# A pool of its own for the first attention, with eleven more buffers for coded weights and a deeper decode lead

## The chip, the cores and the metric

The kernel runs on one core of one Trainium2 chip. The metric is the device time of one execution in microseconds (us). Times are given as the median of several executions; the trace comes from one profiled execution of its own.

## What is computed

Attention with a decaying bias over 2 batches, 8 heads and 576 positions; then a feed-forward layer with an ELU-like activation (2048 hidden); then a mixture of four experts (1024 hidden each) weighted by normalised probabilities.

```python
cum = np.cumsum(np.maximum(s, 0.0), axis=-1)
bias = -(cum[:, :, :, None] - cum[:, :, None, :])
scores = np.where(causal, -1e9, q @ k.T / 8 + np.minimum(bias, 0.0))
x = softmax(scores) @ v                      # 1152 tokens x 512
h = x @ w_in                                 # w_in 512 x 2048
x = np.where(h > 0, h, np.exp(np.minimum(h, 0)) - 1) @ w_out
p = probs / (probs.sum(-1, keepdims=True) + 1e-9)
out = sum(p[:, e:e+1] * (np.maximum(x @ w1[e], 0) @ w2[e]) for e in range(4))
```

## The kernel before

The 1152 tokens are worked in three groups of 256, 448 and 448 (`GROUPS`). The weights come in **units** of 128 hidden columns: a unit is a tile of 128 x 1024, its first 512 columns the block of the up matrix and its last 512 the block of the down matrix. The feed-forward layer has 16 units (`NAB`), the four experts 8 each (`NCD`), 32 in all.

The 16 units of the feed-forward layer arrive as 64-bit integers (`w64`), that is as 32 **coded halves** of 512 KB, each half a unit. `fetch_halves` (L118) issues their loads on the queue of the SP engine (SyncE), in the order of `order` (L103), into buffers borrowed from tags whose real use comes later. `turn` (L106) lists these: one `wu` tile with two halves, three `gt` tiles, and then rounds of `small` with eleven halves (`yh`, `yl`, three `raw`, three in `xa`, three in `ox`). The first sixteen halves so find a free buffer at once; a half of a later round waits until the half before it in the same buffer is decoded. `decode_halves` (L131) turns a half into 32-bit weights with two ScalarE operations (L146, L148) and two VectorE operations (L149, L151), and sends each finished unit to a DRAM tile (`w_dec`, L154, on the GpSimd queue) for the later groups. `DEC` (L46) gives how many halves are decoded at four points within the first attention; afterwards `advance(n)` (L592) decodes up to half 2n + `AHEAD` in slot n.

The first group's attention (`attention_first`, L234) takes only its first 256 positions and stands ahead of everything. It begins with 12 unread products of the identity with itself (`keep_warm`, L330); an fp32 product is two instructions on TensorE. `scores`, `probabilities`, `normalise`, `transposes` and `values` follow for four pairs of heads. `transposes` and `keep_warm` take turns in two PSUM buffers (`ps_att`).

Then `layer1(0, ...)` (L667) runs the feed-forward layer on group 0 in plain fp32, one slot for each unit: `up1`, exponential (L699), `Relu` (L702) and VectorE step (L703) into `gt`, `advance`, and two slots later `down1`. Its PSUM buffers for `up1` are two, so `up1` of slot k waits for L703 of slot k - 2. After slot 3 `sums_hook` calls `cum_parts` (L191), which writes the running sums and their parts to DRAM on ScalarE's DMA queue; its tile `rows` has one buffer and is filled and written twice.

From slot 14 on a `Background` interleaves the attention of group 1 (`attention_parts`, L365): `load_small` and `load` (under `late`, which puts their DMAs behind the last load of a coded half) and `split` (L431), whose loads from `rows_d` (L443, L444) are not under `late`. Then the 32 expert units follow for group 0 (`up2`, `down2`), with `fetch` (L91) four units ahead on the SP queue into `raw`, and `prepare` (L95). Groups 1 and 2 come after that. Each engine and each DMA queue works its instructions in order; the framework's scheduler sets that order, starting from the order of the program but moving instructions forward where it takes an engine to be free.

Of the kernel before, what the change touches and what calls it, by code (L numbers as in the profile page):

```python
# [9 lines left out]
F32R = mybir.dt.float32r  # L10
# [6 lines left out]
B, H, S, D = 2, 8, 576, 64  # L17
# [25 lines left out]
BG_FROM = [14, 0, 0]  # L43
BG_TO = [1, 1, 0]

DEC = [1, 2, 3, 4]  # L46
AHEAD = 6

N_WU, N_GT = 1, 3

@with_exitstack
def tile_kernel(ctx, tc, qT, kT, v, s, w64, w, probs, out):
    nc = tc.nc


    base = ctx.enter_context(tc.tile_pool(name="base", bufs=1, reuse_waits="tile"))

    edge = ctx.enter_context(tc.tile_pool(name="edge", bufs=1, side="right"))
    att_stack, l1_stack = ExitStack(), ExitStack()
    att_pool = att_stack.enter_context(tc.tile_pool(name="att", bufs=1, reuse_waits="tile"))  # L60
    l1_pool = l1_stack.enter_context(
        tc.tile_pool(name="l1", bufs=1, side="right", reuse_waits="tile"))
    psum = ctx.enter_context(tc.tile_pool(name="ps", bufs=1, space=bass.MemoryType.PSUM))
    PE, DVE, ACT, POOL, SP = nc.tensor, nc.vector, nc.scalar, nc.gpsimd, nc.sync
# [5 lines left out]

    def sb(shape, tag, bufs, dtype=F32):
        p = (base if tag in BASE else edge if tag in EDGE else l1_pool if tag in L1
             else att_pool)
        return p.tile(shape, dtype, tag=tag, name=tag, bufs=bufs)

    def ps(tag, bufs):
# [26 lines left out]
    order = [(0, 0)] + [h for n in range(NAB - 1) for h in ((n + 1, 0), (n, 1))] + [(NAB - 1, 1)]  # L103

    small = [("yh", 1, 1), ("yl", 1, 1)] + [("raw", 3, 1)] * 3 + [("xa", 1, 3), ("ox", 1, 3)]
    turn = [("wu", 5, 2)] * N_WU + [("gt", 3, 1)] * N_GT + small * 4  # L106
    places = [(tag, bufs, n, i) for tag, bufs, n in turn for i in range(n)]
    coded, freed_by, last_in = {}, [], {}
    for i, (tag, bufs, many, k) in enumerate(places):
# [81 lines left out]
    def cum_parts():  # L191

        ACT.dma_start(out=cum_d, in_=cum)
        one = sb([B * H, S], "bias", 2)
        POOL.memset(one, 1.0)
        for i in (2, 3):
            ACT.dma_start(out=rows_d[:, i], in_=one)
        for i, sign in ((0, 1.0), (4, -1.0)):
            t = sb([B * H, 2, S], "rows", 1, F32R)
            ACT.activation(t[:, 0], cum, AF.Copy, scale=sign)  # L200
            DVE.scalar_tensor_tensor(out=t[:, 1], in0=cum, scalar=sign, in1=t[:, 0].bitcast(F32),
                                     op0=ALU.mult, op1=ALU.subtract)
            ACT.dma_start(out=rows_d[:, i:i + 2], in_=t.bitcast(F32))
# [30 lines left out]
    def attention_first(x):  # L234


        n = 256
        qkv = sb([128, 3, 4, n], "pt", 2)
        SP.dma_start(out=s_sb, in_=s)
        for c in (0, 2):  # L240
            for i, t in enumerate((qT, kT)):
                SP.dma_start(out=qkv[:, i, c:c + 2], in_=t[0, 128 * c:128 * c + 256, 0:n]
                             .rearrange("(c p) n -> p c n", p=128))
        fetch_halves(1)
        vv = qkv[:, 2].rearrange("p c n -> p (c n)").rearrange("p (c d) -> p c d", c=2)
        SP.dma_start(out=vv, in_=v[0, 0:n].rearrange("(c p) d -> p c d", p=128))
        fetch_halves()
        cum_sums()
        pp = []
        for tag, heads in (("k2", 3), ("k2", 3), ("q2", 1), ("q2", 1)):  # L250
            t = sb([128, heads, 3 * 128], tag, 2)
            pp += [t[:, h] for h in range(heads)]
        ptt = sb([128, H, 3 * 128], "pt", 2)
        sm = sb([128, 2, H], "sm8", 1)


        parts, less = (sb([80, n], t, 1, F32R) for t in ("cump", "cumm"))
        ones = sb([80, B * H], "ones", 1, F32R)
        POOL.tensor_copy(ones[:64], ident[:64, :B * H])
        POOL.tensor_copy(ones[64:], ident[64:80, 64:64 + B * H])  # L260
        for t, sign in ((parts, 1.0), (less, -1.0)):
            POOL.tensor_copy(t[:64], zero)
            ACT.activation(t[:B * H], cum[:, 0:n], AF.Copy, scale=sign)
            DVE.scalar_tensor_tensor(out=t[64:], in0=cum[:, 0:n], scalar=sign,
                                     in1=t[:B * H].bitcast(F32), op0=ALU.mult, op1=ALU.subtract)

        chunks = [(0, 128), (128, 256)]  # L270
        banks = {}

        def scores(hp):
            for j in range(2):
                h = 2 * hp + j
                banks[h] = ps(f"acc{h % 4}", 1) if h < 4 or h > 5 else ps("up", 2)
            for d0, d1 in chunks:
                for j in range(2):
                    r = slice(64 * j, 64 * j + 64)
                    PE.matmul(banks[2 * hp + j][:, d0:d0 + d1], qkv[r, 0, hp, d0:d1],  # L280
                              qkv[r, 1, hp, 0:d1], start=d0 == 0, stop=False,
                              skip_group_check=True)
            for j in range(2):
                h = 2 * hp + j
                one = ones[:, h:h + 1]
                for d0, d1 in chunks:
                    o = banks[h][:, d0:d0 + d1]
                    PE.matmul(o, one.to_broadcast([80, 128]), parts[:, 0:d1],
                              start=False, stop=False, skip_group_check=True)
                    PE.matmul(o, less[:, d0:d1], one.to_broadcast([80, d1]),  # L290
                              start=False, stop=d0 > 0, skip_group_check=True)

        def probabilities(hp):
            for j in range(2):
                h = 2 * hp + j
                for i, (d0, d1) in enumerate(chunks):
                    p = pp[h][:, d0:d0 + d1]
                    nm = sb([128, 1], "nm", 8)
                    DVE.tensor_tensor_reduce(p, banks[h][:, d0:d0 + d1], mask[:, S - d1:],
                                             -1.0 / SC, 3.0e38, ALU.add, ALU.min, nm)  # L300
                    ACT.activation(p, p, AF.Exp, bias=nm, scale=-1.0, accum_out=sm[:, i, h:h + 1])

        def normalise(hp):
            r = sm[:, :, 2 * hp:2 * hp + 2]
            DVE.tensor_scalar(r, r, 1e-9, None, op0=ALU.add)
            DVE.reciprocal(r, r)
            for h in (2 * hp, 2 * hp + 1):
                for i, (d0, d1) in enumerate(chunks):
                    p = pp[h][:, d0:d0 + d1]
                    scaled = DVE.tensor_scalar(p, p, sm[:, i, h:h + 1], None, op0=ALU.mult)  # L310
            return scaled

        def transposes(hp):
            for h in (2 * hp, 2 * hp + 1):
                pt = ps_att()
                for m in range(3):
                    ms = slice(128 * m, 128 * m + 128)
                    PE.transpose(pt[:, ms], pp[h][:, ms], ident)
                ACT.activation(ptt[:, h], pt[:, :384], AF.Copy)

        def values(hp):
            o = ps(f"acc{(hp + 2) % 4}", 1)
            for c, q0 in ((0, 0), (1, 128)):
                for j in range(2):
                    h = 2 * hp + j
                    PE.matmul(o[64 * j:64 * j + 64, q0:n], vv[:, c, 64 * h:64 * h + 64],  # L326
                              ptt[:, h, 256 * c:256 + 128 * c], start=c == 0, stop=c == 1)
            return ACT.activation(x[:, hp], o[:, :n], AF.Copy)

        def keep_warm(products):  # L330


            o = ps_att()[:, :128]
            for _ in range(products):
                last = PE.matmul(o, ident, ident, start=True, stop=True)
            return last

        with tc.issue_after(keep_warm(12).ins):
            for hp in range(3):
                scores(hp)  # L340
        probabilities(0)
        decode_halves(DEC[0])
        scores(3)
        probabilities(1)
        normalise(0)
        transposes(0)
        probabilities(2)
        normalise(1)
        transposes(1)
        values(0)  # L350
        decode_halves(DEC[1])
        probabilities(3)
        normalise(2)
        transposes(2)
        values(1)
        decode_halves(DEC[2])
        last = [normalise(3)]
        transposes(3)
        values(2)
        last.append(values(3))  # L360
        decode_halves(DEC[3])
        return last
# [364 lines left out]
    class First:  # L727
# [3 lines left out]
        def __call__(self, at):  # L731
            if at > BG_FROM[0]:
                if self.got is None:
                    xs[1] = sb([128, 2, NCC, N2], "xa", 1, F32R)
                    self.got = Background(attention_parts(1, xs[1]), BG_FROM[0],
                                          NAB + LAG + E * NCD - BG_TO[0])
                self.got(at)
# [334 lines left out]
```

## Time and profile before

| | us |
|---|---|
| median of 3 runs | 735.73 |
| the runs | 732.92, 735.73, 735.87 |
| the profiled execution | 733.4 |
| its span, first to last instruction | 731.5 |

A row of the trace gives a start, a duration, the engine, the line, the operation with the tiles that it writes and reads, and in square brackets how long the engine had stood idle before it and whose end released it. PE is TensorE's products, PEld its weight loads, DVE VectorE, ACT ScalarE, POOL GpSimd, SPq the queue of SyncE. PEclk is the granted clock of TensorE as a share of 2.4 GHz. A busy PE is a modelled figure: products overlap, and at half the clock each takes about twice as long.

### The profile page before, as it was taken

The numbers are of one execution on the slowest core, as the hardware profiler recorded it, in microseconds if no ns is written. First come the engines' busy times: TensorE is split into PE (matmuls) and PEld (weight loads), VectorE is DVE, ScalarE is ACT, GpSimd is POOL, SyncE is SP. The second block draws the span as 40 slices with busy tenths as digits, with TensorE's granted clock in tenths as the row PEclk, the third lists the DMA queues.
The fourth block names the chain that finished last, engine by engine and source line by source line (L and its number), as shares of the span: only waits on it lengthen the run. The fifth ranks groups of instructions, "written<-read, shape, count | busy, mean of one in ns | idle before, by whom it ended". The sixth has DMA issues, their size and how long they took to land.

```text
span 731.5 us, 10289 instructions
## 1 busy us (share of the span) xinstructions
PE 707.5 (97%) x3650; PEld 600.8 (82%) x3650; DVE 561.2 (77%) x1154; ACT 368.5 (50%) x769; POOL 13.6 (2%) x33
## 2 busy tenths in 40 slices
PE   7989788999999999999999999999999999999997
PEld 5678676878787888787899998888888888888886
DVE  4588566998786888887696549988888888888765
ACT  4688555967675867675754424222222233333220
POOL 2011000000000000000000000000000000000000
PEclk7699998999999999999999999999999999999999
DMA  8669995677566464533553100111111111111002
GB/s 317 237 205 356 363 280 177 191 215 213 159 199 210 146 192 120 149 119 103 201 188 120 39 0 1 59 57 58 59 57 58 58 57 59 58 58 58 1 0 101
DMA packets 41987, 97.00 MB, mean 133 GB/s; under 512 B 5232, under 2 KB 18736, under 8 KB 41936
## 3 DMA queue, kind: packets, MB, share of 16 engines
q1 hardware_dynamic: 39472, 87.69, 36.2%
q0 software_dynamic: 2304, 8.39, 2.9%
q8 instruction: 29, 0.48, 0.3%
q10 hardware_dynamic: 160, 0.26, 0.1%
q14 instruction: 22, 0.18, 0.1%
HBM read 85.32 MB, written 11.01 MB: 132 GB/s over the span
## 4 chain that ended last, share of the span: by engine, by line
PE 85%; DMA 6%; ACT 3%; DVE 3%; issue 1%; SPq 1%; ACTq 0%; DVEq 0%
PE acc L581 37%; PE up L581 16%; PE att L907 10%; PE up L907 8%; PE att L536 3%; PE att L509 3%; DMA pt<-in_qT 2%; PE att L464 1%; PE att L457 1%; DMA v<-in_v 1%; PE att L459 1%; ACT wu L146 1%; DMA wu<-in_w 1%; PE acc L326 1%; DMA raw<-in_w 1%
## 5 line engine op out<-in xcount | busy, mean ns | idle before, releaser
L581 PE MATMUL acc<-w,h 128*128 128x512 f32 x672 | 171.9, 392 | 0.0
L581 PEld LDWEIGHTS acc<-w,h 128*128 128x128 f32 x672 | 126.1, 188 | 23.0 <-ACT h L917 0.2
L83 DVE TENSOR_TENSOR wu<-raw,wu 128x1024 fp32r<-128x1024 f32 x64 | 78.1, 1220 | 19.7 <-ACT wu L99 19.0
L581 PE MATMUL acc<-gt,wu 128*128 128x448 f32 x384 | 87.9, 372 | 0.0
L649 DVE SCALAR_TENSOR_TENSOR ox<-acc,pr,ox 128x512 f32<-128x512 f32 x105 | 78.4, 747 | 11.3 <-PE acc L581 9.2
L917 ACT ACTIVATE h<-c 128x448 fp32r<-128x448 f32 x48 | 27.4, 573 | 111.0 <-DVE c L923 111.0
L99 ACT ACTIVATE wu<-raw 128x1024 fp32r<-128x1024 f32 x64 | 67.5, 1055 | 20.4 <-PE acc L581 13.6
L581 PEld LDWEIGHTS acc<-gt,wu 128*128 128x128 f32 x384 | 70.1, 188 | 7.9 <-issue 2.6
L907 PE MATMUL att<-S,top 128*128 128x448 f32 x288 | 66.3, 365 | 0.0
L907 PEld LDWEIGHTS att<-S,top 128*128 128x128 f32 x288 | 54.0, 188 | 6.7 <-issue 0.2
L581 PE MATMUL acc<-wu,gt 128*128 128x512 f32 x192 | 57.0, 409 | 0.0
L581 PE MATMUL up<-yh,wu 128*128 128x256 f32 x256 | 55.0, 295 | 1.3 <-ACT wu L99 1.3
L581 PEld LDWEIGHTS up<-yh,wu 128*128 128x128 f32 x256 | 43.4, 196 | 4.5 <-issue 1.8
L907 PE MATMUL up<-x2a,top 128*128 128x448 f32 x192 | 44.2, 366 | 0.0
L918 DVE SCALAR_TENSOR_TENSOR h<-c,h 128x448 fp32r<-128x448 f32 x48 | 29.8, 623 | 18.7 <-ACT h L917 18.7
L581 PE MATMUL up<-xa,wu 128*128 128x448 f32 x192 | 43.6, 371 | 0.0
L581 PE MATMUL up<-ox,wu 128*128 128x448 f32 x192 | 41.5, 366 | 0.7 <-DVE e L707 0.7
L695 PE MATMUL up<-xf,wu 128*128 128x256 f32 x128 | 33.3, 401 | 8.3 <-DVE gt L703 8.1
L499 ACT ACTIVATE p<-p,nm 128x384 f32<-128x384 f32 (+4 forms) x56 | 34.5, 616 | 13.2 <-DVE nm L494 12.7
L907 PEld LDWEIGHTS up<-x2a,top 128*128 128x128 f32 x192 | 35.9, 188 | 4.8 <-ACT p L932 0.6
L581 PE MATMUL up<-yl,wu 128*128 128x256 f32 x128 | 37.4, 292 | 2.0 <-DVE yl L83 2.0
L581 PEld LDWEIGHTS up<-ox,wu 128*128 128x128 f32 x192 | 36.0, 188 | 3.9 <-DVE e L707 1.1
(185 smaller groups left out, 1200.3 us busy)
## 6 DMA issues: line engine op xcount, KB each, us to landing
raw<-in_w SPq DMA_DIRECT2D x41, 512.0 KB
raw<-w_dec SPq DMA_DIRECT2D x32, 512.0 KB
raw<-in_w SPq DMA_DIRECT2D x16, 1024.0 KB
w_dec<-wu POOLq DMA_DIRECT2D x16, 512.0 KB, 7.2
k<-in_kT SPq DMA_DIRECT2D x16, 288.0 KB
xa<-in_w SPq DMA_DIRECT2D x6, 512.0 KB
ox<-in_w SPq DMA_DIRECT2D x6, 512.0 KB
cbp<-cum_d SPq DMA_DIRECT2D x16, 144.0 KB
```

Source lines behind the costliest of these rows:

```text
L83: DVE.tensor_tensor(out=lo, in0=x, in1=hi.bitcast(F32), op=ALU.subtract)
L99: ACT.activation(t[:, 0], x, AF.Copy)
L146: ACT.activation(m, high.bitcast(F32), AF.Abs, scale=2.0 ** -112))
L499: ACT.activation(p, p, AF.Exp, bias=nm, scale=-1.0, accum_out=sm)
L509: PE.transpose(pt[:cb[c + 1] - cb[c], m, :], p[:, cb[c]:cb[c + 1]], ident)
L536: PE.matmul(o[64 * j:64 * j + 64, qs:nq], job["v"][:n, c, 64 * j:64 * j + 64], job["pt"][:n, j, c, qs:nq], start=c == 0, stop=c == n_c - 1)
L581: PE.matmul(o, a[m], b[n], start=first and i == 0, stop=last and i == 2)
L649: DVE.scalar_tensor_tensor(out=o_sb, in0=o, scalar=pr[:, i, e:e + 1], in1=o_sb, op0=ALU.mult, op1=ALU.add)
L695: PE.matmul(o, t[:, dm(c)], x[:, c], start=c == 0, stop=c == NCC - 1)
L907: PE.matmul(bank, tops[q][:, m, op, cs], x[:, n, c], start=first and c + i == 0, stop=c == 1 and i == 2, skip_group_check=True)
L917: ACT.activation(h[:, 0, u, cs], c, AF.Relu)
L918: DVE.scalar_tensor_tensor(out=h[:, 1, u, cs], in0=c, scalar=0.0, in1=h[:, 0, u, cs].bitcast(F32), op0=ALU.max, op1=ALU.subtract)
```

## The change

The first attention gets a pool of its own (`first`). Beside its tiles this pool holds eleven new buffers `cd` for one coded half each. `first` is closed when the background begins (after slot 14), and the pool `att`, in which the attention of groups 1 and 2 works, is opened then. In `turn` the eleven `cd` stand behind `gt`, so 27 halves find a free buffer at once, and the remaining five reuse `yh`, `yl` and `raw`. The fourth `DEC` goes from 4 to 5 and `AHEAD` from 6 to 10. The tile of `cum_parts` takes the tag `k2` with two buffers in place of `rows` with one. Two more groups of unread products, 6 and 4, are put behind the last scores and behind the first transposes.

```diff
-DEC = [1, 2, 3, 4]
-AHEAD = 6
-N_WU, N_GT = 1, 3
+DEC = [1, 2, 3, 5]
+AHEAD = 10
+N_WU, N_GT, N_CD = 1, 3, 11
...
-    att_stack, l1_stack = ExitStack(), ExitStack()
-    att_pool = att_stack.enter_context(tc.tile_pool(name="att", bufs=1, reuse_waits="tile"))
+    first_stack, att_stack, l1_stack = ExitStack(), ExitStack(), ExitStack()
+    att_pool = [first_stack.enter_context(
+        tc.tile_pool(name="first", bufs=1, reuse_waits="tile"))]
...
-             else att_pool)
+             else att_pool[0])
...
-    turn = [("wu", 5, 2)] * N_WU + [("gt", 3, 1)] * N_GT + small * 4
+    turn = [("wu", 5, 2)] * N_WU + [("gt", 3, 1)] * N_GT + [("cd", N_CD, 1)] * N_CD + small * 2
...
-            t = sb([B * H, 2, S], "rows", 1, F32R)
+            t = sb([B * H, 2, S], "k2", 2, F32R)
...
         decode_halves(DEC[0])
-        scores(3)
+        with tc.issue_after(scores(3).ins):
+            keep_warm(6)
         probabilities(1)
         normalise(0)
-        transposes(0)
+        with tc.issue_after(transposes(0).ins):
+            keep_warm(4)
...
             if at > BG_FROM[0]:
                 if self.got is None:
+                    first_stack.close()
+                    att_pool[0] = att_stack.enter_context(
+                        tc.tile_pool(name="att", bufs=1, reuse_waits="tile"))
                     xs[1] = sb([128, 2, NCC, N2], "xa", 1, F32R)
```

`scores` and `transposes` now return their last instruction, which `issue_after` needs.

## Rows read from the trace of the kernel before

**Rows 1.** The page: busy time of TensorE, its share of the span, instructions.
```profile
PE 707.5 (97%) x3650; PEld 600.8 (82%) x3650; DVE 561.2 (77%) x1154; ACT 368.5 (50%) x769; POOL 13.6 (2%) x33
```

**Rows 2.** Busy time by stretch: engines' busy us (instructions), granted clock, DMA share, GB/s.
```profile
11.30:30.00 18.70, 18.70 (x78) 13.55 (x79) 10.44 (x53) 10.91 (x38) 0.00 (x0) 0.50 0.97 382
29.30:44.30 15.00, 12.33 (x66) 8.03 (x65) 9.52 (x29) 11.61 (x26) 0.68 (x1) 0.97 0.11 40
38.70:103.30 64.60, 56.52 (x249) 48.23 (x249) 50.47 (x105) 48.87 (x108) 7.98 (x15) 0.95 0.89 311
44.30:114.00 69.70, 59.88 (x273) 51.04 (x271) 48.44 (x101) 45.55 (x103) 7.98 (x15) 0.95 0.99 329
88.60:94.90 6.30, 5.02 (x12) 4.03 (x13) 4.80 (x10) 6.14 (x16) 0.53 (x1) 0.50 1.07 298
115.70:122.20 6.50, 6.17 (x25) 5.22 (x25) 5.73 (x20) 4.30 (x13) 0.00 (x0) 0.50 0.49 153
122.20:731.50 609.30, 604.60 (x3181) 517.64 (x3179) 483.06 (x948) 291.60 (x583) 0.00 (x0) 1.00 0.31 102
```

**Rows 3.** Timeline of TensorE, 38 to 116 us: products that waited, and one more.
```profile
42.28 1.99 PE L695 MATMUL up<-xf,wu 128*128 128x256 f32 x8 [2.42 <-DVE gt L703]
...
45.84 1.89 PE L695 MATMUL up<-xf,wu 128*128 128x256 f32 x8
...
60.83 1.99 PE L695 MATMUL up<-xf,wu 128*128 128x256 f32 x8 [1.02 <-DVE gt L703]
...
89.88 3.78 PE L695 MATMUL up<-xf,wu 128*128 128x256 f32 x8 [4.61 <-DVE gt L703]
...
106.09 0.38 PE L581 MATMUL up<-yl,wu 128*128 128x256 f32 x1 [2.00 <-DVE yl L83]
...
113.41 0.33 PE L459 MATMUL att<-kl,qb 68*128 68x128 f32 x1 [1.92 <-DMA qb<-rows_d]
...
114.99 0.38 PE L581 MATMUL up<-yh,wu 128*128 128x256 f32 x1 [1.26 <-ACT wu L99]
```

**Rows 4.** Timelines of ScalarE and VectorE: first slots, and two long waits.
```profile
40.99 0.69 ACT L146 ACTIVATE wu<-gt 128x512 f32<-128x512 f32 x1
41.55 0.40 ACT L699 ACTIVATE e<-up 128x256 f32<-128x256 f32 x1
...
43.94 0.42 DVE L703 SCALAR_TENSOR_TENSOR gt<-up,e 128x256 f32<-128x256 f32 x1
...
58.98 0.68 ACT L200 ACTIVATE rows<-cum 16x576 fp32r<-16x576 f32 x1 [3.17 <-DMA rows_d<-rows]
...
88.76 0.31 ACT L448 ACTIVATE qb<-pt 64x128 fp32r<-64x128 f32 x1 [6.06 <-DMA pt<-in_qT]
```

**Rows 5.** The chain of work that ended last: its long DMA pieces (start, us).
```profile
53.36 5.60 DMA rows_d<-rows
...
72.02 16.72 DMA pt<-in_qT
...
98.33 8.53 DMA v<-in_v
```

**Rows 6.** Prices: the unread products (timeline), decode steps (by line: ns min/median/max).
```profile
1.84 5.00 PE L335 MATMUL att<-ident 128*128 128x128 f32 x24 [1.84 <-POOL ident masks.py:199]
...
L146 ACT ACTIVATE wu<-raw x9: 649/663/698, 43.9 to 92.7; 128x512 f32<-128x512 f32 x9
...
L148 ACT ACTIVATE z<-raw x9: 647/658/703, 41.9 to 91.0; 128x512 int32<-128x512 uint32 x9
...
L149 DVE SCALAR_TENSOR_TENSOR wu<-wu,z x32: 668/684/693, 15.5 to 93.4; 128x512 int32<-128x512 int32 x32
```

**Rows 7.** Timeline of the SP queue: issues of coded halves (L127) and what follows.
```profile
17.30 2.87 SPq L127 DMA_DIRECT2D ox<-in_w  x3
...
43.50 0.34 SPq L127 DMA_DIRECT2D yh<-in_w  x1
...
68.75 3.17 SPq L127 DMA_DIRECT2D raw<-in_w  x3
72.02 2.18 SPq L389 DMA_DIRECT2D pt<-in_qT  x2
...
94.78 0.33 SPq L93 DMA_DIRECT2D raw<-in_w  x1
```

More of the change, by code (lines that the diff above doesn't have):

```diff
@@ L289, in scores @@
                               start=False, stop=False, skip_group_check=True)
-                    PE.matmul(o, less[:, d0:d1], one.to_broadcast([80, d1]),
-                              start=False, stop=d0 > 0, skip_group_check=True)
+                    last = PE.matmul(o, less[:, d0:d1], one.to_broadcast([80, d1]),
+                                     start=False, stop=d0 > 0, skip_group_check=True)
+            return last
         def probabilities(hp):
@@ L317, in transposes @@
                     ms = slice(128 * m, 128 * m + 128)
-                    PE.transpose(pt[:, ms], pp[h][:, ms], ident)
+                    last = PE.transpose(pt[:, ms], pp[h][:, ms], ident)
                 ACT.activation(ptt[:, h], pt[:, :384], AF.Copy)
+            return last
         def values(hp):
```

## The prediction

> **What bounds the kernel now.** The page comes first: TensorE is busy for 97% of the span [rows 1], so there is little to win but where it stands still or runs at half its clock. The table of stretches says where that is. From 122.2 us to the end TensorE is busy for 604.6 of 609.3 us at full clock [rows 2]; whatever the change saves before 122 us arrives at the end, and nothing that it does later matters. Before 122 us there are three places. From 11.3 to 30 us, in the first attention, the clock stands at 0.50, that is 1.2 GHz, with TensorE busy all the time by the model [rows 2]. From 38.7 to 103.3 us, the feed-forward layer on group 0, TensorE is busy for 56.5 of 64.6 us [rows 2]. After that, up to 115 us, it waits again.
>
> TensorE's own timeline gives the waits: 2.42 us before 42.28, 1.02 before 60.83, 4.61 before 89.88, 2.00 before 106.09, 1.92 before 113.41 and 1.26 before 114.99 [rows 3]. Twice the clock is at 0.50 afterwards: from 88.6 to 94.9 us with 5.02 us of busy time and from 115.7 to 122.2 us with 6.17 us [rows 2]. At full clock that work would take half, so this cost about 2.5 and 3.1 us.
>
> Then what stands behind the waits. The first is VectorE and ScalarE with decoding. The second is ScalarE at L200, held for 3.17 us by the write of the single `rows` tile [rows 4], a DMA of 5.60 us in the chain [rows 5]. The third is ScalarE at L448, which waited 6.06 us for the `load_small` DMA [rows 4]; the exponentials and `Relu`s queue behind it, and so L703 and TensorE. That DMA took 16.72 us from issue to landing [rows 5]. It is issued at 72.02, right behind the last coded halves [rows 7]. The last three waits are on loads too, two of them through VectorE and ScalarE, and the chain runs there over the load of `v`, 8.53 us [rows 5]. The DMA columns say why the loads are late: between 29.3 and 44.3 us the engines of the DMA are busy for 11% at 40 GB/s, between 44.3 and 114.0 us for 99% at 329 GB/s [rows 2]. The SP queue shows the same: the sixteenth coded half is issued by 20.2 us, the seventeenth only at 43.50, when a buffer came free [rows 7]. **The stretch up to 114 us is bound by transfers that could have run in an idle gap.**
>
> **The change part by part.** *Eleven `cd` buffers.* Eleven halves of 0.524 MB, 5.8 MB, can run in the gap. 27 halves and the 1.6 MB of the attention's inputs (by their shapes) are 15.7 MB, at the 382 GB/s of the first stretch [rows 2] 41 us, so they land by about 44 us; the gap is filled to its end. The stretch behind it loses 5.8 MB, at 329 GB/s [rows 2] 17.5 us of transfer. Loads that landed between 89 and 114 us can land some 15 us earlier, while TensorE will come to its need for them only some 5 us earlier (4.61, 2.5 and 1.0 less what the start costs, below). The last halves are issued when halves 16 to 20 are decoded, which with the new lead is slots 4 to 6, some 60 us, in place of 72; `load_small` follows then. So I count the waits of 4.61, 2.00, 1.92 and 1.26 us as gone, and with them both falls of the clock, 2.5 and 3.1: **-15.4 us**. Lower bound of this gain: the loads of the experts (L93) need `raw` buffers, which coded halves hold until slots 10 and 11, so the second set of waits can stay. Then only 4.61 and 2.5, that is 7.1, are won.
>
> *The second buffer for the parts of the sums.* L200 no longer waits, so TensorE's 1.02 us go: **-1.0 us**, with the first attention's readers of `k2` long done by slot 3. SP's loads from `rows_d` come earlier as well, which the part above needs.
>
> *Four halves more of lead.* In each of the first slots the next exponential stands behind the decodes of the slot before: the sixth L146 starts at 40.99 and the second exponential at 41.55 [rows 4], where 2 x 0 + 6 is six. With a lead of ten, four more halves stand before that exponential. A half is 0.66 + 0.66 us on ScalarE and twice 0.68 on VectorE [rows 6], so 5.3 and 5.5 us. L703 of slot 1 then ends up to 5.5 us after its 44.36 [rows 4], and `up1` of slot 3, which needs it, starts at 45.84 now [rows 3]: 1.5 us of that are covered. Part of one half is done earlier, by `DEC`, and ScalarE has some 3.4 us without work between 29.3 and 44.3 [rows 2], of which a part can take decodes. So between 0 and 4.0 us; I take **+2.5**, nearer to the upper end, since ScalarE's order followed the program in the rows that I read. From then on a slot's decoding, 2.7 us on either engine, and its exponential, `Relu` and L703 fit into some 3.5 us, the time of a slot's `up1` and `down1`, two groups of 8 products of up to 1.89 us [rows 3] that overlap a little: ScalarE's 48.9 and VectorE's 50.5 us of work in 64.6 [rows 2] still fit into some 59. The lead is not paid back later, because TensorE sets the pace then. If the new idle time at 45 us lets the clock fall, it costs what it cost at 88.6, 2.5 us; that is kept for the range.
>
> *Ten unread products.* Twelve products are 24 instructions in 5.00 us [rows 6], 0.21 us each. So 6 products are 2.5 us and 4 are 1.7, on TensorE in the first attention. There the chain runs through TensorE, so the whole 4.2 us could lie on the path. Against it stand that the clock may rise earlier than at 30 us: of the 5.7 us between the end of the last scores (about 24.3) and 30, at most half, 2.9 us, can be won back; and that TensorE hands over to engines which then have the decodes of the last part to do anyway, so that a delay of the first exponential is idle time in which ScalarE decodes. Between -1 and +4.2; I take **+1.0**, because the two delays overlap.
>
> The Trainium skill, "TensorE: Matmul & The Clock Gate", Part 4, says that a transpose on TensorE doesn't count as activity for the clock as a product does; by that rule the added products would be what lifts the clock. The trace is in keeping with it so far as TensorE stayed at 0.50 for 18.7 us of modelled busy time [rows 2], but small products stood there too, so it doesn't settle it.
>
> *Pools.* `att` now opens at slot 14 over memory of `first`; its loads wait for the readers of what lay there. The last `cd` is decoded by slot 3, the attention's own tiles before slot 0. Nothing: 0.
>
> **Sum.** -15.4 - 1.0 + 2.5 + 1.0 = -12.9 us. The profiled execution took 733.4 us, so 720.5 us on its scale. It lay 2.3 us below the median of the runs shown; on the scale of the median that is **722.8 us**.
>
> **The rivals.**
>
> *Cheap start.* The clock rises by 27 us and the added decoding hides in ScalarE's idle time; the start costs -1 in place of +3.5. That gives -17.4, 718.3 us; if the wait of 2.42 us goes too and the clock gives back the whole 2.9, some 714, and 712 on the scale of the profiled execution. For it speaks that ScalarE is busy for only 10.9 of 18.7 us in the first attention [rows 2], against it that ScalarE follows the program's order.
>
> *Half of it.* The waits between 104 and 115 us stay, since expert loads and the attention's jobs still come in one burst; only 7.1 + 1.0 is won and 3.5 paid: 731.1 us.
>
> *The change doesn't do what it says.* Eleven more loads are issued early, but decoding, held back by ScalarE and VectorE, sets when the last halves, and with them `load_small`, may go. With the gain of L200 against the start this gives 734 to 738 us, no change.
>
> *Slower.* The place is the head of the SP queue. The expert loads need `raw` buffers that coded halves hold, and an issue that waits there holds all behind it: before, the L93 at 94.78 [rows 7] stands between parts of the attention's loads. If the scheduler puts the first L93 ahead of `load_small`, SP waits until half 29 is decoded in slot 10, about 76 us, later than the 72.02 of now, and the waits of 4.61 and of the 104 to 115 us all stay, while the start is paid: +3.5 to +8, less 1.0, so 738 to 743 us. It decides at the point where L93's first issue precedes L389's. Against it: before, L389 comes first, and its release comes earlier now.
>
> **How the numbers follow.** Forecast 0.50 (717 to 729 us), cheap start 0.17, half of it 0.17, no effect 0.07, slower 0.09. The first three are faster by over 0.5% (under 732.0), except for the upper edge of the half case: 0.82 faster. About 0.5% is what a measurement of this kernel tells from no change. Within 0.5%: 0.09. Slower: 0.09. The range reaches from the best of the cheap start, 712 us, over the half case with a fall of the clock at the start, 733.5 us.
>
> **What would show it.** Right: the first 27 L127 issued without a break up to about 40 us and the DMA's share near 1 from 30 to 43 us; L389 issued near 62 us, L448 with no wait; no stretch at 0.50 after 45 us; L200 without idle time; the second exponential 3 to 5 us later than 41.55 and TensorE waiting before the `up1` of slot 3. Wrong: a wait of ScalarE at L448 or of VectorE at L229 of over 2 us, an L93 ahead of L389, or a clock of 0.50 near 50 us. If the last 609 us change by more than 2 us, the scheduler has reordered later stages, which I don't count on.

## The result, and the profile after

The changed kernel takes 726.82 us (median of 4 runs, 725.66 to 728.23) against 734.77 us for the kernel before, run on the same chip. The ratio is 0.9895, with a 95% interval of 0.9865 to 0.9925: faster by 1.1%, some 8 us, where the prediction said 13. Run again beside the later experiments it came to 0.9897 (0.9875 to 0.9919).

The profiled execution is the slowest of the four, 728.23 us with a span of 726.4. Over the ten executions of the changed kernel on record the time goes with the mean granted clock, from 728.85 us at 0.980 to 725.24 at 0.988, and both its profiles are executions at 0.980, so they show more of the slow clock than the median has. The page gives TensorE almost the same work as in [rows 1]:

```profile
PE 706.4 (97%) x3670; PEld 601.7 (83%) x3670; DVE 561.1 (77%) x1154; ACT 368.5 (51%) x769; POOL 13.6 (2%) x33
```

The table of stretches, with the columns of [rows 2]. First the kernel after:

```profile
29.30:44.30 15.00, 13.57 (x87) 9.96 (x86) 10.26 (x22) 13.69 (x29) 1.75 (x3) 1.00 0.90 357
44.30:64.00 19.70, 17.73 (x68) 15.11 (x69) 19.25 (x40) 17.85 (x37) 3.19 (x6) 0.83 0.80 247
64.00:103.30 39.30, 35.67 (x162) 29.72 (x160) 25.25 (x53) 24.15 (x58) 3.72 (x7) 1.00 1.03 327
103.30:122.20 18.90, 17.12 (x102) 14.21 (x103) 15.55 (x57) 15.85 (x50) 0.00 (x0) 0.91 0.44 151
122.20:726.40 604.20, 599.46 (x3143) 513.42 (x3143) 476.15 (x920) 283.45 (x558) 0.00 (x0) 1.00 0.31 101
45.80:52.30 6.50, 6.03 (x14) 4.87 (x15) 6.43 (x13) 6.34 (x14) 1.37 (x3) 0.50 1.03 306
107.40:110.50 3.10, 3.10 (x17) 3.10 (x16) 2.65 (x13) 1.89 (x8) 0.00 (x0) 0.50 0.19 75
```

And three stretches of the kernel before that do not stand in [rows 2]:

```profile
44.30:64.00 19.70, 18.68 (x87) 16.11 (x86) 16.27 (x33) 15.71 (x33) 3.19 (x6) 1.00 0.98 359
64.00:103.30 39.30, 34.69 (x152) 29.63 (x150) 28.73 (x57) 28.06 (x66) 4.79 (x9) 0.91 0.97 330
103.30:122.20 18.90, 13.35 (x67) 10.91 (x65) 10.16 (x32) 7.61 (x22) 0.00 (x0) 0.82 0.79 209
```

The gap of [rows 2] is filled: 357 GB/s in place of 40 between 29.3 and 44.3 us. That is 4.8 MB more (317 GB/s x 15 us). But a new hole stands behind it: from 44.3 to 64 us the DMA moved 247 GB/s in place of 359, 2.2 MB less. From 64 to 103 us it is as full as ever, 327 against 330 GB/s. **The clock and the loads both changed places**: the slow stretches from 88.6 and from 115.7 us [rows 2] are gone, and new ones at 0.50 stand at 45.8 us and, shorter, at 107.4.

In this timeline and those below, rows between the ones shown are left out. TensorE's timeline: the products that waited, the added unread products (L339), and the product group of slot 4 (52.88):

```profile
24.36 2.77 PE L339 MATMUL att<-ident 128*128 128x128 f32 x12
28.35 1.26 PE L339 MATMUL att<-ident 128*128 128x128 f32 x8
39.61 1.99 PE L701 MATMUL up<-xf,wu 128*128 128x256 f32 x8 [0.46 <-DVE gt L709]
46.27 3.78 PE L701 MATMUL up<-xf,wu 128*128 128x256 f32 x8 [2.94 <-DVE gt L709]
52.88 1.89 PE L701 MATMUL up<-xf,wu 128*128 128x256 f32 x8
78.30 1.99 PE L701 MATMUL up<-xf,wu 128*128 128x256 f32 x8 [1.08 <-DVE gt L709]
91.38 1.99 PE L701 MATMUL up<-xf,wu 128*128 128x256 f32 x8 [1.83 <-DVE gt L709]
104.17 0.33 PE L465 MATMUL att<-kl,qb 68*128 68x128 f32 x1 [0.94 <-DMA kl<-rows_d]
```

The wait of 2.42 us before slot 2 [rows 3] has shrunk to 0.46, the one of 1.02 is gone, and of 4.61, 2.00, 1.92 and 1.26 us there remain 1.08, 1.83 and 0.94 (one of 0.57 at 95.83 is not shown). New is 2.94 us before slot 3, with the slow clock behind it.

ScalarE's and VectorE's timelines, the rows that answer to [rows 4] (L202 is the former L200, L454 the former L448, L101 the former L99):

```profile
44.08 0.37 ACT L705 ACTIVATE e<-up 128x256 f32<-128x256 f32 x1
45.80 0.42 DVE L709 SCALAR_TENSOR_TENSOR gt<-up,e 128x256 f32<-128x256 f32 x1
52.92 1.24 ACT L202 ACTIVATE k<-cum 16x576 fp32r<-16x576 f32 x2
75.04 0.51 ACT L454 ACTIVATE qb<-pt 64x128 fp32r<-64x128 f32 x2 [3.17 <-DMA pt<-in_qT]
88.67 1.06 ACT L101 ACTIVATE wu<-raw 128x1024 fp32r<-128x1024 f32 x1 [3.08 <-DMA raw<-in_w]
```

The second exponential starts at 44.08 in place of 41.55, behind the decoding. ScalarE fills the tile of the sums (L202) twice in a row with no wait. It still waits for the small loads, 3.17 us in place of 6.06, and VectorE waits for the attention's `cbp`, as the view of its waits from 20 to 125 us shows (total, times, longest; L231 is the former L229):

```profile
DVE bias L231 <- DMA cbp<-cum_d: 4.7, 2, 2.5
```

SP's timeline, answering to [rows 7] (L129 the former L127, L395 the former L389, L95 the former L93):

```profile
28.94 2.84 SPq L129 DMA_DIRECT2D xa<-in_w  x3
42.02 1.28 SPq L129 DMA_DIRECT2D ox<-in_w  x3
59.66 0.37 SPq L129 DMA_DIRECT2D yh<-in_w  x1
62.55 3.98 SPq L129 DMA_DIRECT2D raw<-in_w  x3
66.62 1.42 SPq L395 DMA_DIRECT2D pt<-in_qT  x2
82.64 0.33 SPq L95 DMA_DIRECT2D raw<-in_w  x1
83.02 0.60 SPq L417 DMA_DIRECT2D k<-in_kT  x1
```

And two lines of what SP waited for up to 125 us (total, times, longest):

```profile
SPq L129 <- DMA cum_d<-cum: 10.2, 1, 10.2
SPq L95 <- DVE wu L153: 9.4, 2, 6.7
```

Between the loads into `xa` and `ox` SP stood for 10.2 us at the write of `cum_d`, which is issued on ScalarE's queue only at 37.24 and lands at 42.00. At 75.9 us it stood for 6.7 us at the first expert load, L95, until the half in that `raw` buffer was decoded; the attention's load of `k` waited behind it.

### The profile page after: what moved, and what is told of

Its sections match the earlier page's. It is cut to its first block, busy times and chain, and to the rows that moved or that the text cites. A ratio compares the mean times of both kernels' runs of the same rounds, so it can differ in the third digit from the quotient of the medians.

```text
span 726.4 us, 10330 instructions
## 1 busy us (share of the span) xinstructions
PE 706.4 (97%) x3670; PEld 601.7 (83%) x3670; DVE 561.1 (77%) x1154; ACT 368.5 (51%) x769; POOL 13.6 (2%) x33
## 4 chain that ended last, share of the span: by engine, by line
PE 86%; DMA 5%; DVE 3%; ACT 2%; issue 2%; SPq 1%; ACTq 0%; DVEq 0%
PE acc L587 38%; PE up L587 16%; PE att L916 11%; PE up L916 8%; PE att L542 3%; PE att L515 3%; DMA raw<-in_w 2%; PE att L470 1%; PE att L463 1%; DMA pt<-in_kT 1%; PE att L465 1%; DMA wu<-in_w 1%; ACT wu L148 1%; DMA ox<-in_w 1%; DMA cum_d<-cum 1%
## 5 line engine op out<-in xcount | busy, mean ns | idle before, releaser
L101 ACT ACTIVATE wu<-raw 128x1024 fp32r<-128x1024 f32 x64 | 67.5, 1055 | 25.0 <-PE acc L587 17.5
L927 DVE SCALAR_TENSOR_TENSOR h<-c,h 128x448 fp32r<-128x448 f32 x48 | 29.8, 623 | 18.7 <-ACT h L926 18.7
L705 ACT ACTIVATE e<-up 128x448 f32<-128x448 f32 (+1 forms) x48 | 23.3, 485 | 32.6 <-PE up L587 30.9
```

Source lines behind the costliest of these rows:

```text
L101: ACT.activation(t[:, 0], x, AF.Copy)
L705: ACT.activation(e, o, AF.Exp)
L927: DVE.scalar_tensor_tensor(out=h[:, 1, u, cs], in0=c, scalar=0.0, in1=h[:, 0, u, cs].bitcast(F32), op0=ALU.max, op1=ALU.subtract)
```

## Where the time was won

One row serves as a ruler for every run: the first product of group 1, which the timeline of TensorE shows as `up<-xa`. From it to the end of the span it is 493.8 us before (731.5 - 237.72) and 493.9 after (726.4 - 232.52), and in all runs below between 493.7 and 494.2, but 495.3 in e2 and e4. So the profiles differ almost only ahead of that row. The start of the products of slots 2 and 4 divides the time before it:

| kernel | slot 2 | slot 4 | group 1 | slot 4 to group 1 |
|---|---|---|---|---|
| before | 42.28 | 49.29 | 237.72 | 188.4 |
| after | 39.61 | 52.88 | 232.52 | 179.6 |
| after, again | 39.78 | 51.53 | 233.16 | 181.6 |
| e1, lead six | 39.37 | 46.38 | 228.79 | 182.4 |
| e2, no `cd` | 39.03 | 49.24 | 237.09 | 187.9 |
| e3, no added products | 39.17 | 50.91 | 228.68 | 177.8 |
| e4, `raw` free early | 39.71 | 52.95 | 227.41 | 174.5 |
| e6, e4 with lead six | 37.62 | 44.63 | 226.39 | 181.8 |
| e7, products in the gap | 39.41 | 49.64 | 228.14 | 178.5 |
| e8, e4 and e7 | 38.51 | 48.74 | 221.93 | 173.2 |
| e9, e8 less added products | 40.94 | 51.33 | 223.44 | 172.1 |
| b1, two buffers alone | 42.69 | 51.39 | 239.05 | 187.7 |
| b2, lead alone | 40.21 | 51.89 | 234.85 | 183.0 |
| b3, `cd` and two buffers | 42.48 | 49.50 | 230.69 | 181.2 |

In the two profiles the change won 2.7 us up to slot 2, lost 6.3 from there to slot 4, and won 8.8 behind it: 5.2 us in all. Profiles of one kernel vary, so the times below are compared by their medians and ratios.

What stands ahead of slot 2 is in part the clock. In every profile it is at 1.00 at first, falls to 0.50 between 9.6 and 12.7 us, about the time at which TensorE waits for `cump` (3.60 us up to 11.30 in the kernel before), and rises again between 26 and 31 us. The slow stretch lasts 20.5 us in the kernel before, b1 and b3, 13.7 in e3, e6 and e8 and 17.1 in the other eight. The earlier it begins, the longer it lasts: from 9.6 to 10.1 us in the first three, from 12.5 to 12.7 in the second. Between the kernel before and the changed one the 3.4 us of difference are worth some 1.7 us, an estimate by half of them, out of the 2.7. The three long ones are the kernels whose fourth `DEC` is 4, and they are also the last to reach slot 2; whether that `DEC` or chance made them long no run shows.

| kernel | median (us) | ratio to before (95%) |
|---|---|---|
| after, again | 727.06 | 0.9897 (0.9875 to 0.9919) |
| e1 | 725.88 | 0.9871 (0.9845 to 0.9896) |
| e2 | 732.58 | 0.9972 (0.9956 to 0.9989) |
| e3 | 725.55 | 0.9876 (0.9856 to 0.9897) |
| e4 | 724.28 | 0.9858 (0.9826 to 0.9891) |
| e6 | 724.76 | 0.9853 (0.9821 to 0.9884) |
| e7 | 724.38 | 0.9868 (0.9844 to 0.9891) |
| e8 | 717.85 | 0.9771 (0.9749 to 0.9793) |
| e9 | 719.35 | 0.9785 (0.9766 to 0.9805) |
| b1 | 734.87 | 1.0001 (0.9986 to 1.0017) |
| b2 | 731.11 | 0.9964 (0.9948 to 0.9980) |
| b3 | 726.98 | 0.9889 (0.9872 to 0.9906) |

## The experiments: one part at a time

**The two buffers of the sums alone (b1).**

```diff
-            t = sb([B * H, 2, S], "rows", 1, F32R)
+            t = sb([B * H, 2, S], "k2", 2, F32R)
```

> The kernel before with one part of the change alone: the tile of the running sums has two buffers. By the prediction's step this is worth -1.0 us (ScalarE's 3.17 us of waiting at L200 and TensorE's 1.02 us before 60.83 go). If the 16-us wait for the first small DMA decides in any case, the saved microsecond is waited for at slot 11 again and the time is that of before, 0 +- 1 us; both are near what the comparison can tell, so the trace decides: L200 with no idle time, and whether the wait before slot 11 is longer than 4.61 us.

Measured: 1.0001; the interval reaches from -1.0 to +1.2 us, so no gain is seen, though a microsecond is not quite excluded. The timelines of ScalarE and of TensorE in b1:

```profile
52.70 1.24 ACT L200 ACTIVATE k<-cum 16x576 fp32r<-16x576 f32 x2
...
91.98 3.56 PE L695 MATMUL up<-xf,wu 128*128 128x256 f32 x8 [4.46 <-DVE gt L703]
```

The wait at L200 is gone; the 4.61 us before 89.88 [rows 3] answer to 4.46 here, with another 1.17 us before 83.80. The prediction's -1.0 was counted on top of the load waits. That a microsecond saved ahead of a wait for a load is waited for there is in keeping with these rows, but b1's profile does not show it by itself: from slot 4 to group 1 it takes 0.8 us less than the kernel before, and it lost 1.7 us more ahead of that, where its clock fell after slot 2.

**The deeper lead alone (b2).**

```diff
-DEC = [1, 2, 3, 4]
-AHEAD = 6
+DEC = [1, 2, 3, 5]
+AHEAD = 10
```

> The kernel before with the deeper lead alone (DEC's fourth 5, lead ten), with no cd buffers. If the lead is only a cost at the start, as the prediction has it (+2.5 us, with a clock fall +5), the time is 736 to 740 us. The rival: decoding earlier also frees the sixteen buffers earlier, so that the loads of halves 17 to 32 start some 4 to 6 us sooner in the idle gap of 29 to 44 us; this is a small prefetch of its own and gives back 2 to 5 us of the later waits, so the time is 732 to 735 us.

Measured: 0.9964, a gain of 1 to 4 us, and the interval excludes the cost. SP's timeline in b2 shows what goes with it:

```profile
51.80 1.80 SPq L127 DMA_DIRECT2D xa<-in_w  x3
...
65.04 2.75 SPq L127 DMA_DIRECT2D raw<-in_w  x3
67.88 1.99 SPq L389 DMA_DIRECT2D pt<-in_qT  x2
```

Halves that are decoded sooner free their buffers sooner, and between 29.3 and 44.3 us the DMA moves 86 GB/s in place of 40: the last coded loads go out at 65.04 in place of 68.75 and L389 at 67.88 in place of 72.02 [rows 7]. **A deeper decode lead is itself a prefetch.** The table has both sides: slot 4 starts 2.6 us later than before, and from there to group 1 it takes 5.4 us less. The wait for the first small load did not shrink (TensorE's 4.61 us before 89.88 answer to 6.42 before 87.10 here); what went are the later waits and the slow clock at 115.7. And 2.1 us of what b2's profile gains stand ahead of slot 2, where its slow clock lasted 17.1 us in place of 20.5, so what the prefetch alone is worth is not shown.

**The `cd` buffers with the two buffers of the sums (b3).** This is the changed kernel with the old `DEC` and `AHEAD` and without both groups of added products:

```diff
-DEC = [1, 2, 3, 5]
-AHEAD = 10
+DEC = [1, 2, 3, 4]
+AHEAD = 6
...
-        with tc.issue_after(scores(3).ins):
-            keep_warm(6)
+        scores(3)
...
-        with tc.issue_after(transposes(0).ins):
-            keep_warm(4)
+        transposes(0)
```

> The changed kernel without the deeper lead (six, fourth DEC 4) and without the added unread products: the cd buffers and the two buffers of the sums alone. By the prediction's sum these two parts alone are worth -16.4 us, so 718 us. By the traces so far (the changed kernel with a lead of six 725.9, without the products 725.6, both near the changed kernel's 727) the two costs are worth 1 to 2 us together and the native layer still waits for its loads: 723 to 726 us.

Measured: 0.9889, 726.98 us: as much as the whole change. The sum had -16.4 us for these two parts; without the lead they are worth about 8. ScalarE still waits at L452 (the former L448) for `pt<-in_qT`:

```profile
81.13 0.31 ACT L452 ACTIVATE qb<-pt 64x128 fp32r<-64x128 f32 x1 [3.90 <-DMA pt<-in_qT]
```

TensorE waits 1.51 us before 82.25, 2.86 before 96.30 and 1.63 before 100.19, and the clock is at 0.50 from 95.7 to 105.7 us. b3 is not a clean price of the -15.4, which counted on the new lead for the time of the last halves: without it `load_small` (L393, the former L389) goes out at 70.68, against 66.62 in the changed kernel. e3 below has the lead too: -13.9 us by the sum, and -9.1 measured.

**The change without the `cd` buffers (e2).**

```diff
-    turn = [("wu", 5, 2)] * N_WU + [("gt", 3, 1)] * N_GT + [("cd", N_CD, 1)] * N_CD + small * 2
+    turn = [("wu", 5, 2)] * N_WU + [("gt", 3, 1)] * N_GT + small * 4
```

> The changed kernel without the eleven cd buffers (rounds of the small buffers in their place); own pool, lead of 10, two buffers for the sums' parts and unread products stay. Theory A (the early transfers are the gain): the DMA stands still from 30 to 44 us again, the deeper lead waits for loads, and the time is at or above that of the kernel before, 733 to 742 us. Rival C (the gain comes from the second buffer and the clock in the first attention): 725 to 730 us.

Measured: 732.58 us; the buffers are worth 5.5 us to the changed kernel (0.9972 - 0.9897 of 734.8), and the intervals don't touch. In e2 the DMA moved only 114 GB/s between 29.3 and 44.3 us, and TensorE waited once for 9.8 us:

```profile
PE up L701 <- DVE gt L709: 15.9, 5, 9.8
```

The parts do not add up: b2 and b3 (which holds b1's part) together would give -2.6 - 8.2 = -10.8 us, and the change, with the added products, gives -7.6. That the lead and the buffers fill in part the same gap is in keeping with the 86 GB/s of b2 there and the 114 of e2.

**The change with a lead of six (e1), and without the added products (e3).**

```diff
-AHEAD = 10
+AHEAD = 6
```

> The changed kernel with AHEAD back at 6, all else as changed. Theory A (the deeper lead is a cost at the start, and with the early loads it is not needed): the wait of 2.94 us before the up products of slot 3 at 46.27 us and the stretch at half clock behind it (45.8 to 52.3 us) go, so the first slots end some 4 to 6 us earlier; half 16 is decoded two slots later, so the last five coded loads and load_small come some 5 us later relative to the slots and take back up to 4 us: 721 to 727 us, 0 to 6 below the changed kernel. Theory B (the lead is what brings the last five loads and load_small forward, and so most of the gain): 729 to 735 us.

> The changed kernel without the two added groups of unread products. The prediction put them at +1.0 us (TensorE's time on the path), by which this kernel would be 1 us faster. Rival (the trace after: the clock rises at 28.3 in place of 30.0 us and the third up products start at 39.6 in place of 42.3): it is 1 to 2.5 us slower, its clock rising near 30 us. Between the two (within 1 us): ScalarE's decoding behind it swallows the difference.

e3 takes both groups of products out, as in b3. Measured: 725.88 and 725.55 us, each 1 to 2 us below the changed kernel, with intervals that touch its own; neither part is told from nothing. The rows under e1 are clear all the same: slot 4 starts at 46.38 in place of 52.88, and no wait stands before slot 3, but ScalarE waits 6.18 us at L454 and TensorE 3.46 before 83.49. So the lead costs 6.5 us in the profile, the fall of the clock included, and gives back 2.8 of it behind slot 4.

As to the products: the slow clock of the first attention lasted 13.7 us in e3 and 17.1 in b2 and e9, all without them, 13.7 or 17.1 in the kernels with them, and 20.5 in the kernel before, b1 and b3, again without them. So they are not needed for a short one. The Trainium skill, "TensorE: Matmul & The Clock Gate", Part 4, says that transposes don't count as activity for the clock as products do, which would make the added products what lifts it. That the rule holds here is not shown, nor excluded. The prediction took the 18.7 us at 0.50 to be in keeping with it, but up to 24.05 us of them TensorE ran products alone, without a transpose (L280, L288 and L290 of the kernel before).

## The experiments: what stands in the way of the rest

Two things in the profile after were not in the sum as costs: coded halves that hold `raw`, and the gap before slot 3.

**`raw` free early (e4).** `small` comes ahead of `cd`, so that the first halves lie in `raw` and are decoded first, and the last five halves go into `yh`, `yl` and `xa`:

```diff
-    turn = [("wu", 5, 2)] * N_WU + [("gt", 3, 1)] * N_GT + [("cd", N_CD, 1)] * N_CD + small * 2
+    turn = [("wu", 5, 2)] * N_WU + [("gt", 3, 1)] * N_GT + small + [("cd", N_CD, 1)] * N_CD
+    turn += [("yh", 1, 1), ("yl", 1, 1), ("xa", 1, 3)]
```

> The changed kernel with the same buffers in another order: the eleven halves of small ahead of the eleven cd, and the last five halves in yh, yl and xa, none in raw. So raw is free after half 9, and the last five wait only for halves 5, 6 and 10 to 12. Theory D (in the changed kernel the rest of the expected gain is lost at the head of the SP queue: an expert load waits 6.7 us for a raw buffer that half 29 holds, the attention's loads behind it): the last coded load is issued by 52 us in place of 66.5, load_small lands by 65 us, no wait of ScalarE over 1 us at L454 or at the expert loads' L101, so TensorE's waits of 1.08, 1.83 and 0.57 us and about half of the loss from 103 to 111 us go: 720 to 723 us. Rival E (the loss is that ScalarE and VectorE have too much decoding to do, not the loads): within 1.5 us of the changed kernel.

> As the one before, with AHEAD back at 6 as well. If the early loads and the cost of the lead are separate (theories A and D both): the sum of both steps, 716 to 720 us, with no stretch at half clock between 40 and 100 us. If the deeper lead is needed to keep TensorE supplied (theory B): 724 us or more, with TensorE waiting for VectorE's L709 in several slots.

Measured: 724.28 us, 2.9 us below the changed kernel by the ratios, and 724.76 with a lead of six (e6); both intervals touch that of the changed kernel. The stretch with the hole, and SP's timeline in e4:

```profile
44.30:64.00 19.70, 17.64 (x68) 14.96 (x69) 18.44 (x32) 17.99 (x38) 3.19 (x6) 0.83 0.99 378
```

```profile
53.24 4.32 SPq L95 DMA_DIRECT2D raw<-in_w  x3
61.58 6.21 SPq L396 DMA_DIRECT2D pt<-in_qT  x2
```

The first three expert loads go out from 53.24, where the first went at 82.64, L396 (the former L395) at 61.58. The hole between 44.3 and 64 us is closed, with 378 GB/s in place of 247. From slot 4 to group 1 it takes 174.5 us in place of 179.6. The wait of 2.94 us before slot 3 and the slow clock behind it stay. e6 has neither and reaches slot 4 8.3 us earlier than e4, but takes 7.3 us more from there to group 1, with waits of 1.08 us before 77.14 and 2.18 before 87.36 among it. But the order of SP's queue differs between the two as well. In e6 the fourth expert load stands ahead of `load_small`, and SP waits 20.6 us at it:

```profile
76.78 0.34 SPq L95 DMA_DIRECT2D raw<-in_w  x1
77.23 1.55 SPq L396 DMA_DIRECT2D pt<-in_qT  x2
```

`load_small` so goes out 15.7 us later than in e4. This is the order that the prediction's rival "slower" feared. How much of the 7.3 us is the lead and how much this order is not shown.

**Products in the gap (e7).** 13 unread products stand behind the `down1` of the first unit, which runs in slot 2, where TensorE then waits for L709 (`last_down` holds the last product of `down1`):

```diff
+        if k == 2:
+            o = ps_att()[:, :128]
+            with tc.issue_after(last_down[0].ins):
+                for _ in range(13):
+                    PE.matmul(o, ident, ident, start=True, stop=True)
```

> The changed kernel with 13 unread products more (26 instructions of 0.107 us, 2.8 us) on TensorE between the down products of slot 2 and the up products of slot 3, where it stands idle for 2.94 us and the clock falls behind it. If the fall of the clock is a cost of its own (3.0 us from the half clock between 45.8 and 52.3 us): 1.5 to 3 us below the changed kernel, no stretch at 0.50 between 40 and 60 us. If what TensorE loses there is given back by the loads' lateness further on: within 0.7 us.

Measured: 724.38 us, 2.1 us below the changed kernel by the ratios; the intervals touch. The stretch at 45.8 us and TensorE's timeline in e7:

```profile
45.80:52.30 6.50, 6.50 (x33) 5.50 (x32) 6.06 (x15) 6.47 (x15) 1.06 (x2) 1.00 1.04 353
```

```profile
42.97 3.06 PE L758 MATMUL att<-ident 128*128 128x128 f32 x26
45.87 1.89 PE L702 MATMUL up<-xf,wu 128*128 128x256 f32 x8
49.64 1.99 PE L702 MATMUL up<-xf,wu 128*128 128x256 f32 x8
```

The products fill the gap and nothing else: slot 3 starts at 45.87, against 46.27 without them, the clock stays at 1.00, and slot 4 starts 3.2 us earlier. Later ScalarE waits 5.76 us for `pt<-in_qT`, until 79.30, and TensorE 2.93 us before 81.99, with the clock at 0.50 from 83.1 to 86.5: part of what the start won is waited for there.

**Both (e8), and both without the change's own added products (e9).**

> The early free raw buffers (as in e4_free_raw) and the 13 unread products in the gap together. If the loads were what hid the clock's cost in the changed kernel, the two add up here: 720 to 722.5 us, 2 to 4 below e4_free_raw. If TensorE is bound by ScalarE and VectorE up to 230 us: as e4_free_raw, 723.5 to 725 us.

> The version with raw freed early and with 13 unread products in the gap of slot 3 (717.85 us), without the two added groups of unread products in the first attention. If these are a plain cost on the path, as in the run of the changed kernel without them (-1.5 us, not told from zero), the time is 716 to 717 us. If they are what makes the clock rise in time, the clock rises later and the time is 719 to 722 us.

e8 is e4's and e7's edit together, e9 is e8 with e3's. Measured: 717.85 and 719.35 us, 0.9771 and 0.9785 of before. e8's interval lies below those of e4 and e7, so each of the two edits gains where the other is in place. Its stretches, and all of TensorE's waits of 38 to 122 us:

```profile
44.30:64.00 19.70, 19.40 (x93) 16.28 (x92) 18.16 (x37) 17.27 (x37) 2.69 (x6) 1.00 1.01 403
64.00:103.30 39.30, 39.17 (x200) 34.38 (x199) 30.20 (x74) 27.94 (x67) 3.72 (x7) 1.00 0.77 254
```

```profile
PE up L703 <- DVE gt L711: 0.9, 2, 0.7
PE acc L588 <- ACT gt L796: 0.2, 1, 0.2
PE up L588 <- DVE sm L479: 0.2, 1, 0.2
```

The clock is full from 31 to 122 us, and the DMA is no longer full from 64 to 103 us: 254 GB/s. This is what the prediction described for the change itself. SP stands for 8.3 us at the write of `cum_d` in e8 too, with no wait of TensorE of over 0.7 us behind it. e8 and e9 are not told apart. **e8 beats both kernels**, at 717.85 us against 726.82 and 734.77.

By the ratios e4 and e7 win 2.9 and 2.1 us and both together 9.3; by the rulers of the profiles they win 5.1, 4.4 and 10.6, nearly a sum. But the profile of the changed kernel lies 1.4 us above its median, which counts twice in the sum and once in the 10.6, and e4 takes 1.4 us more behind the ruler. With both taken off, 2.3 and 3.0 stand against 9.2. That is the picture of the ratios; how much the two gain over their sum stays uncertain.

## Why the prediction was right, and where not

The direction was right and 726.8 lies in the range, 4 us above the forecast and close to the middle between it and the rival "half of it" (731.1). By its own signs the mechanism was right in part only. ScalarE's wait at L454 (3.17 us), VectorE's at L231 (2.5 us at the longest) and the clock of 0.50 near 50 us are three of the signs that it named for being wrong. The early issue of `load_small`, L202 without idle time, the wait before slot 3 and the unchanged last stretch are signs for being right. Step by step:

- **What bounds the kernel: right.** The stretch behind the ruler is unchanged within 0.1 us in the two profiles, and loads that could run in an idle gap held it up: e2 against the change shows it for 5.5 us.
- **The gap filled: right, but for the break.** 357 GB/s; the loads did break off for 10.2 us at `cum_d`, where the prediction saw the 27 halves run through. Between 31.8 and 42.0 us SP issued nothing at all. The Trainium skill, "DMA: Bandwidth & Descriptors", section "Anatomy of one DMA — SWDGE (gpsimd) path", says that a wait for a semaphore happens on the issuing sequencer ahead of dispatch; the trace agrees, here for SP's queue. Why a load into `ox` waits for the write of `cum_d` no run shows.
- **"I count the waits as gone, and with them both falls of the clock: -15.4" is the term that was mis-sized.** b3, which has the buffers of this term and the two of the sums, measured -8.2 us for -16.4; e3, which has the lead as well, -9.1 for -13.9. The issue times were nearly right: the last halves 59.66 to 66.5 us, L395 at 66.62 where "near 62" was said. What failed is the conclusion from issue to landing: the DMA is still full from 64 to 103 us, with a hole ahead of it, so the small loads are waited for (3.17 us), and SP is held at L95. There half 29 was decoded at 82.6 us, where the prediction had about 76. The prediction had this as the lower bound of the gain and as a rival, "half of it", with a chance of 0.17. e8 against e7, 7.1 us by the ratios, shows that the places of the last coded halves cost this much; what of it is the hole and what the hold at L95 is not separated, since e4's edit ends both. Of 4.61, 2.00, 1.92, 1.26, 2.5 and 3.1 us there stay 1.08, 1.83, 0.57, 0.94 and some 1.6 for the clock (half of 3.10 us busy at 0.50): 6.0 of 15.4.
- **The lead, +2.5: right at its place, wrong in the sum.** Between e1 and e2, whose profiles have no slow clock there, slot 4 starts 2.9 us later with the lead of ten (e2 also lacks the `cd` buffers); the second exponential comes 2.5 us later than before. The fall of the clock, which was kept for the range, came in the profile and cost 3.0 us (half of 6.03). "The lead is not paid back later, because TensorE sets the pace then" is the step that failed: TensorE did not set the pace, loads did, and the lead frees their buffers. Alone it goes with a gain (b2), in the change it comes to nothing that can be told.
- **Two buffers, -1.0: no gain seen alone** (b1), with -1.0 at the edge of the interval. Load waits of 4.46 and 1.17 us still stood behind them.
- **Added products, +1.0: in keeping** with e3 (-1.5 us without them) and with e9 (+1.5), and so not told from nothing.
- **The rival "slower"** described SP's head rightly and its order wrongly: L95 came behind L395, so it held only what came after. In e6 the order is the feared one.

Against b3's -8.2, the load waits and the two buffers were given 8 us too much (-16.4); between b3 and the change, -7.6, the lead and the products cost 0.6, where 3.5 was said. The two errors partly cancel, and leave the 5 us between -12.9 and -7.6. That the lead gives back part of what the load waits keep was in no term of the sum, so it is in part luck that the total came this near; with the lead's cost as it was put, the forecast would have lain some 8 us off.

## What to carry to other kernels

When loads are moved into an idle gap, follow the last of them to its landing, and look at what its buffers hold up: here the 4.8 MB that moved into the gap did not settle the gain, since the loads behind the burst and the head of their queue still made the engines wait. Parts that shorten the same stretch need not add: by the ratios e4 and e7 brought 2.9 and 2.1 us alone and 9.3 together, when no long wait was left. A lead in decoding is paid on the engines and can be repaid through the buffers that it frees; weigh both.

## What the runs showed that was not expected

- A wait of nearly the same length was followed by either clock. After 2.94 us before 46.27 the changed kernel's clock stood at 0.50 for 6.5 us; e2, after 2.93 us, stayed at 1.00 for as long, as its rows show:

```profile
45.68 1.99 PE L701 MATMUL up<-xf,wu 128*128 128x256 f32 x8 [2.93 <-DVE gt L709]
```

```profile
45.70:52.20 6.50, 6.50 (x30) 5.75 (x31) 6.50 (x14) 6.47 (x14) 1.06 (x2) 1.00 0.99 331
```

Of the six profiles with a wait of 2.7 to 2.94 us before slot 3 the clock fell behind it in five, all but e2; of the eight without one it stood at 1.00 there in all but b1, which fell after 2.42 us before slot 2. After the same 2.42 us the kernel before stayed up [rows 3].
- The slow stretch in the first attention did not follow the added products: it ended at 26.3 us in e3, which has none, and at 28.6 in the changed kernel, which has ten. Kernels that are alike up to there differ too, 28.6 us in e4 and 26.2 in e8.
- Work that does nothing can be worth its time: with 26 instructions, 3.06 us in a gap that was there in any case, the slow stretch that cost 3.0 us did not come in any of the three profiles that have them (e7, e8, e9).
